# Cosine attention and a feed-forward layer in one kernel: input loads reordered, batch 1's q prepared at once, x in two buffers

## The chip, the cores and the metric

The kernel runs on one core of a Trainium2 chip. The metric is the device time of one execution in microseconds (us). TensorE (PE in the profile) multiplies matrices, VectorE (DVE) and ScalarE (ACT) do elementwise work, GpSimd (POOL) here only issues transfers, and SyncE (SP) issues DMA transposes. Weight loads of TensorE have a row of their own (PEld).

## The reference

```python
def phi(x, c, s):                       # x: (batch, head, seq, 64)
    r = np.maximum(x, 0.0)
    return np.concatenate([r * c, r * s], axis=-1)
q_p = phi(q, cos_w, sin_w)              # cos_w, sin_w depend on the position alone
k_p = phi(k, cos_w, sin_w)
kv  = np.einsum('bhsf,bhsd->bhfd', k_p, v)
z   = np.sum(k_p, axis=2)
num = np.einsum('bhsf,bhfd->bhsd', q_p, kv)
den = np.einsum('bhsf,bhf->bhs', q_p, z)[..., None] + 1e-06
attn = num / den
...
x = attn.transpose(0, 2, 1, 3).reshape(8 * 576, 512)
h = x @ w_in                            # (4608, 512) @ (512, 2048)
g = h * (1.0 / (1.0 + np.exp(-1.702 * h)))
out = g @ w_out                         # (4608, 2048) @ (2048, 512)
```

There are 8 batches of 8 heads with 576 positions of 64 values. All inputs and the output are float32 in memory; the kernel computes in bfloat16 with float32 sums.

## The kernel before

The 4,608 tokens are worked on in nine blocks of 512 (`i`). Each block multiplies by `w_in` (mm1, 16 groups `fc`), applies the activation, and multiplies by `w_out` (mm2). Beside block `i` the attention of batch `i + 1` is done in small pieces, at places given by `at(n, ...)`, where `n` counts 32 steps of a block: 16 of mm1, then 16 of mm2. A batch has 576 rows, so five pieces: four "mains" of 128 rows, that come in one transfer, and a "tail" of 64 rows, in a transfer of its own. Transfers that change the type from float32 to bfloat16 go through GpSimd's queue (the "cast queue"):

```python
    def load_main(b, n):
        state[b][n] = t = two.tile([128, 2048], BF16, name=n)
        nc.gpsimd.dma_start(out=t.rearrange("p (h e) -> p h e", h=H),
                            in_=SRC[n][b, :, 0:512, :].rearrange("h (p c) d -> p h (c d)", c=4))

    def load_tail(b, n, on=None, dt=BF16):
        state[b][n, 4] = t = two.tile([64, 512], dt, name=n + "t" + str(dt == F32))
        (on or nc.gpsimd).dma_start(out=t.rearrange("p (h d) -> p h d", h=H),
                                    in_=SRC[n][b, :, 512:576, :].rearrange("h p d -> p h d"))
    # ... (load_w_in(g), load_w_out(g): quarter g of w_in or w_out, 1 MB of float32, on the cast queue)
    load_tail(0, "k", nc.sync, F32)
    load_tail(0, "v", nc.sync, F32)
    load_main(0, "q")
    # ... (index patterns on GpSimd between the loads)
    load_main(0, "k")
    load_main(0, "v")
    for g in range(4):
        load_w_in(g)
    load_main(1, "q")
    load_tail(1, "q")
    load_tail(0, "q")
    load_w_out(0)
    for n in "kv":
        load_main(1, n)
        load_tail(1, n)
    for g in range(1, 4):
        load_w_out(g)
    load_all(2)                     # q, k and v of batch 2, mains and tails
```

Each piece of q is prepared by VectorE into `qn` and turned by a DMA transpose into `qT`; the tail of batch 0 has a place of its own, `qT_tail`. `unit_kv` makes the small matrix of a batch, `unit_num` the rows of x of one piece in `xb`, and `turn_x` turns them by a DMA transpose into `xT`, which mm1 reads. `qn`, `qT`, `xT`, `kp` and `vt` have one buffer:

```python
    def prep_new(b):
        state[b]["qn"] = one.tile([128, NC, H, 2 * D], BF16, name="qn")
        state[b]["xb"] = one.tile([128, NC, H, D], BF16, name="xb")

    def prep(b, n, c):
        o = state[b]["qn"] if n == "q" else kp
        for cs, w in enumerate((cosw, sinw)):
            nc.vector.tensor_scalar(o[:rows(c), c, :, cs * D:cs * D + D], part(b, n, c), 0.0, w[:rows(c), c:c + 1],
                                    op0=MAX, op1=MUL)
    # ...
    def turn_q(b, c):
        nc.sync.dma_start_transpose(out=q_slot(b, c)[:, :, 0:rows(c)],
                                    in_=state[b]["qn"][:rows(c), c].rearrange("p h e -> p (h e)"))

    def turn_x(b, c):
        nc.sync.dma_start_transpose(out=xT[:, :, ds(b * S + c * 128, rows(c))],
                                    in_=state[b]["xb"][:rows(c), c].rearrange("p h d -> p (h d)"))
    # ...
    def unit_num(b, c):
        nm = at_tile()
        for h in range(H):
            nc.tensor.matmul(nm[:, h // 4, ds(h % 4 * (D + 1), D + 1)], q_slot(b, c)[:, h, :],
                             state[b]["kvs"][:, h // 4, h % 4, 0:D + 1], start=True, stop=True)
        # ... den and inv from nm, on VectorE
        nc.vector.tensor_tensor(state[b]["xb"][:r, c].rearrange("p (n h) d -> p n h d", n=2), nm4[:, :, :, 0:D],
                                inv[:r].unsqueeze(3).to_broadcast([r, 2, 4, D]), op=MUL)
```

Batch 0 is prepared before the first block, with transposes of q and x on TensorE for the four mains, and with matmuls on a constant tile (`warmup`) while TensorE waits. Then follows the loop. In block 0 mm2 goes through the four quarters of `w_out` in turn, each for the four token tiles, so that it can begin with the first quarter:

```python
    warmup(18)
    # ... q of batch 0: prepared, turned on TensorE through two `at` banks, copied to qT by ScalarE
    for c in (4, 0, 1, 2, 3):
        prep(0, "k", c)
    for c in (4, 0, 1, 2, 3):
        prep_v(0, c)
    warmup(14)
    unit_kv(0)
    # ... unit_num(0, 0..3), x turned on TensorE, the first four groups of mm1 of block 0
    for i in range(NBLK):
        # ...
        if i == 0:
            at(4, prep, 0, "q", 4)
            at(4, turn_q, 0, 4)
            at(9, unit_num, 0, 4)
            at(9, turn_x, 0, 4)
        elif i + 2 < B:
            at(1, load_all, i + 2)
        if b < B:                                   # b = i + 1
            k0, k1, k2 = (5, 17, 19) if i == 0 else (0, 12, 17)
            at(k0, prep_new, b)
            for c in range(NC):
                at(k0 + c // 2, prep, b, "q", c)
                at(k0 + c // 2, turn_q, b, c)
                at(k0 + 5 + c // 2, prep, b, "k", c)
                at(k0 + 9 + c // 3, prep_v, b, c)
            at(k1, unit_kv, b)
            for c in range(NC):
                at(k2 + 2 * c, unit_num, b, c)
                at(k2 + 2 * c, turn_x, b, c)
        for n in range(32):
            if n < FC:                              # FC = 16
                if i > 0 or n > 3:
                    mm1(i, n)
            elif i == 0:
                mm2(i, n % 4, (n - FC) // 4)        # token tile, quarter of w_out
            # ...
            else:
                mm2(i, (n - FC) // 4, n % 4)
            for f in work[n]:
                f()
```

Of the kernel before, what the change touches and what calls it, by code (L numbers as in the profile page):

```python
# [9 lines left out]
F32 = mybir.dt.float32  # L10
BF16 = mybir.dt.bfloat16
# [10 lines left out]
def kernel(  # L22
# [9 lines left out]
    nc = tc.nc  # L32
    B, H, S, D = q.shape
# [6 lines left out]
    NC = 5  # L40
# [3 lines left out]
    one = ctx.enter_context(tc.tile_pool(name="one", bufs=1))  # L44
    two = ctx.enter_context(tc.tile_pool(name="two", bufs=2))
# [7 lines left out]
    def rows(c):  # L53
        return 128 if c < 4 else 64
# [4 lines left out]
    def mm_tile():  # L59
        return ps.tile([128, TB], F32, name="mm", bufs=4)  # L60

    def at_tile():
        return ps.tile([128, 2, 512], F32, name="at", bufs=2)

    def warmup(n):
        for _ in range(n):
            wps = mm_tile()
            nc.tensor.matmul(wps, warm[:, 0:128], warm, start=True, stop=True)  # L68


    state = {b: {} for b in range(B)}
    SRC = {"q": q, "k": k, "v": v}

    def load_main(b, n):
        state[b][n] = t = two.tile([128, 2048], BF16, name=n)
        nc.gpsimd.dma_start(out=t.rearrange("p (h e) -> p h e", h=H),
                            in_=SRC[n][b, :, 0:512, :].rearrange("h (p c) d -> p h (c d)", c=4))

    def load_tail(b, n, on=None, dt=BF16):
        state[b][n, 4] = t = two.tile([64, 512], dt, name=n + "t" + str(dt == F32))  # L80
        (on or nc.gpsimd).dma_start(out=t.rearrange("p (h d) -> p h d", h=H),  # L81
                                    in_=SRC[n][b, :, 512:576, :].rearrange("h p d -> p h d"))

    def load_all(b):
        for n in "qkv":
            load_main(b, n)
            load_tail(b, n)
# [6 lines left out]
    def load_w_in(g):  # L94
        nc.gpsimd.dma_start(out=w_in_sb[:, :, ts(g, 512)], in_=win_r[:, :, ts(g, 512)])

    def load_w_out(g):
        nc.gpsimd.dma_start(out=w_out_sb[:, ts(g, 4), :], in_=wout_r[:, ts(g, 4), :])

    pos_i = const.tile([128, NC], I32)  # L100
    id_i = const.tile([128, 128], I32)
    load_tail(0, "k", nc.sync, F32)
    load_tail(0, "v", nc.sync, F32)
    load_main(0, "q")
    nc.gpsimd.iota(pos_i[:, 0:4], pattern=[[1, 4]], base=0, channel_multiplier=4)
    nc.gpsimd.iota(pos_i[:, 4:5], pattern=[[1, 1]], base=512, channel_multiplier=1)
    load_main(0, "k")
    nc.gpsimd.iota(id_i, pattern=[[1, 128]], base=0, channel_multiplier=-1)
    load_main(0, "v")
    for g in range(4):  # L110
        load_w_in(g)
    load_main(1, "q")
    load_tail(1, "q")
    load_tail(0, "q")
    load_w_out(0)
    for n in "kv":
        load_main(1, n)
        load_tail(1, n)
    for g in range(1, 4):
        load_w_out(g)  # L120
    load_all(2)

# [6 lines left out]
    qT = one.tile([128, H, NC * 128], BF16, name="qT")  # L129
# [9 lines left out]
    ident = const.tile([128, 128], BF16)  # L139
# [11 lines left out]
    def part(b, n, c):  # L151
        if c < 4:
            return state[b][n].rearrange("p (h c d) -> p c h d", c=4, d=D)[:, c]
        return state[b][n, 4].rearrange("p (h d) -> p h d", d=D)

    def prep_new(b):
        state[b]["qn"] = one.tile([128, NC, H, 2 * D], BF16, name="qn")
        state[b]["xb"] = one.tile([128, NC, H, D], BF16, name="xb")

    def prep(b, n, c):  # L160
        o = state[b]["qn"] if n == "q" else kp
# [4 lines that stand above are left out]
    def prep_v(b, c):  # L166
        nc.vector.tensor_copy(vt[:rows(c), c, :, 0:D], part(b, "v", c))

    def q_slot(b, c):

        return qT_tail if (b, c) == (0, 4) else qT[:, :, ts(c, 128)]
# [4 lines that stand above are left out]
# [6 lines left out]
    def unit_kv(b):  # L182
        kv = at_tile()
        for h in range(H):
            o = kv[:, h // 4, ds(h % 4 * (D + 1), D + 1)]
            for c in range(NC):
                nc.tensor.matmul(o, kp[:, c, h, :], vt[:, c, h, 0:D + 1], start=(c == 0), stop=(c == NC - 1))  # L187
        kvs = two.tile([128, 2, 4, VW], BF16, name="kvs")
        for n in range(2):
            o, i = kvs[:, n, :, 0:D + 1], kv[:, n, 0:4 * (D + 1)].rearrange("p (h e) -> p h e", h=4)  # L190
            if b == 0 and n == 1:
                nc.scalar.copy(o, i)
            else:
                nc.vector.tensor_copy(o, i)  # L194
        state[b]["kvs"] = kvs
# [28 lines left out]
    def mm1(i, fc):  # L224
        hps = mm_tile()
        mm1_part(hps, i, fc)
        gelu(hps, fc)
# [17 lines left out]
    def mm2(i, t, part):  # L245

        if part == 0:
            cur[t] = mm_tile()
        yps = cur[t]
        for fc in range(part * 4, part * 4 + 4):  # L250
            nc.tensor.matmul(yps, gT[fc][:, ds(t * 128, 128)], w_out_sb[:, fc, :],  # L251
                             start=(fc == 0), stop=(fc == FC - 1))
        if part == 3 and (i > 0 or t < 3):
            evac(i, t)
# [10 lines left out]
    def mm2_last(i, t):  # L265

        yps = mm_tile()
        ysb = ypool.tile([128, d_model], F32, name="ysb")
        hd = d_model // 2
        for n in range(2):  # L270
            cols = ds(n * hd, hd)
            if n == 1:
                yps = mm_tile()
            for fc in range(FC):
                nc.tensor.matmul(yps[:, 0:hd], gT[fc][:, ds(t * 128, 128)], w_out_sb[:, fc, cols],  # L275
                                 start=(fc == 0), stop=(fc == FC - 1))
            if n == 0:
                nc.scalar.copy(ysb[:, cols], yps[:, 0:hd])
            else:
                nc.vector.tensor_copy(ysb[:, cols], yps[:, 0:hd])  # L280
            for m, (p0, cnt, row, step) in enumerate(pieces(i * 4 + t)):
                (nc.sync if m == 0 else nc.scalar).dma_start(out=out[row:row + (cnt - 1) * step + 1:step, cols],
                                                             in_=ysb[p0:p0 + cnt, cols])


    prep_new(0)
    s0 = state[0]
    warmup(18)
    for c2 in range(2):
        tp = at_tile().bitcast(BF16)  # L290
        for c in (2 * c2, 2 * c2 + 1):
            prep(0, "q", c)
            for h in range(H):
                nc.tensor.transpose(tp[:, c % 2, ts(h, 128)], s0["qn"][:, c, h, :], ident)
            nc.scalar.copy(qT[:, :, ts(c, 128)], tp[:, c % 2].rearrange("p (h t) -> p h t", h=H))
    for c in (4, 0, 1, 2, 3):
        prep(0, "k", c)
    for c in (4, 0, 1, 2, 3):
        prep_v(0, c)
    warmup(14)  # L300
    unit_kv(0)
    tp = [mm_tile().bitcast(BF16) for _ in range(2)]

# [25 lines left out]
    for i in range(NBLK):  # L329
        work = {n: [] for n in range(32)}  # L330
        b = i + 1

        def at(n, f, *a):
            work[n].append(lambda: f(*a))

        if i == 0:
            at(4, prep, 0, "q", 4)
            at(4, turn_q, 0, 4)
            at(9, unit_num, 0, 4)
            at(9, turn_x, 0, 4)  # L340
        elif i + 2 < B:
            at(1, load_all, i + 2)
        if b < B:
            k0, k1, k2 = (5, 17, 19) if i == 0 else (0, 12, 17)
            at(k0, prep_new, b)
            for c in range(NC):
                at(k0 + c // 2, prep, b, "q", c)
                at(k0 + c // 2, turn_q, b, c)
                at(k0 + 5 + c // 2, prep, b, "k", c)
                at(k0 + 9 + c // 3, prep_v, b, c)  # L350
            at(k1, unit_kv, b)
            for c in range(NC):
                at(k2 + 2 * c, unit_num, b, c)
                at(k2 + 2 * c, turn_x, b, c)
        for n in range(32):
            if n < FC:
# [3 lines that stand above are left out]
                mm2(i, n % 4, (n - FC) // 4)  # L360
            elif i == NBLK - 1 and n >= 28:
                if n == 28:
                    mm2_last(i, 3)
# [5 lines that stand above are left out]
            evac(i, 3, nc.vector)  # L369
# [30 lines left out]
```

## Time and profile before

The median of three runs is 315.57 us (315.48 to 317.07).

| of the profile | value |
|---|---|
| span of the profiled execution | 315.0 us |
| PE busy | 286.2 us, 91% |
| DVE, ACT, POOL busy | 103.5, 115.9, 97.3 us |
| mm1 (line 216) | 128.5 us |
| mm2 (line 251) | 128.7 us |
| mean granted TensorE clock | 0.973 |
| cast queue (q0) | 43,904 packets, 27.40 MB |
| sync queue (q1) | 52,672 packets, 12.99 MB |

The profile counts a line of idle time to what ended it. "PE at L200 <- DVE den L206: 8.0, 1, 8.0" says that TensorE, before it wrote the tile `at` on line 200, waited 8.0 us in total, once, 8.0 us at the longest, for an instruction of VectorE on line 206. A transfer appears as "DMA out<-in". In the list of DMA queues, q0 is the cast queue and q1 the sync queue, each with packets, megabytes moved, and the share of time of 16 DMA engines. `qtFalse` in the profile is the tail of q in bfloat16, `ktTrue` and `vtTrue` are the two float32 tails of batch 0. The granted clock is a share of full speed.

### The profile page before, as it was taken

What the parts mean: (1) busy time and instruction counts of PE and PEld (TensorE: products, weight loads), DVE (VectorE), ACT (ScalarE), POOL (GpSimd) and SP (SyncE); (2) the same over time, 40 slices, a digit from 0 to 9 for tenths busy, and PEclk for the clock granted to TensorE, in tenths of its full rate; (3) what the DMA queues carried; (4) which work ended last, traced back from release to release, by engine and by line L of the source; (5) the groups of instructions that cost most, each with busy time, mean ns of one, the idle gap of its engine ahead of it and who ended that gap; (6) DMA issues with size and microseconds to landing.
All of it is one profiled execution on the core that took longest, in us unless ns stands there. A gap on an engine that the chain in (4) does not pass through costs nothing.

```text
span 315.0 us, 4917 instructions
## 1 busy us (share of the span) xinstructions
PE 286.2 (91%) x1867; PEld 143.6 (46%) x1900; DVE 103.5 (33%) x347; ACT 115.9 (37%) x193; POOL 97.3 (31%) x115
## 2 busy tenths in 40 slices
PE   7479697089997999999999999999999999999994
PEld 2356252044553455445544554455445544444443
DVE  2851370057435602740472048015902500000000
ACT  4516330006521463155216512641363146316511
POOL 8633420008011941291049015701610220011021
PEclk9998798779999999999999999999999999999999
DMA  7999999937999999599869977995750640011023
GB/s 104 201 206 195 191 190 165 152 69 181 138 149 185 148 156 170 127 203 172 131 116 186 178 116 140 196 177 100 149 113 0 121 89 0 32 70 34 0 62 73
DMA packets 96759, 40.83 MB, mean 130 GB/s; under 512 B 65568, under 2 KB 94496, under 8 KB 96736
## 3 DMA queue, kind: packets, MB, share of 16 engines
q0 software_dynamic: 43904, 27.40, 58.3%
q1 hardware_dynamic: 52672, 12.99, 28.8%
q8 instruction: 15, 0.25, 0.3%
q10 hardware_dynamic: 160, 0.13, 0.1%
q14 instruction: 8, 0.07, 0.1%
HBM read 36.70 MB, written 9.44 MB: 146 GB/s over the span
## 4 chain that ended last, share of the span: by engine, by line
PE 72%; DMA 18%; SPq 3%; DVE 3%; ACT 1%; issue 1%; POOL 0%; DVEq 0%; ACTq 0%; POOLq 0%
PE mm L251 34%; PE mm L216 33%; DMA qtFalse<-in_q_dram 5%; DMA qT<-qn 4%; SPq L174 3%; PE at L200 3%; DMA k<-in_k_dram 3%; DMA xT<-xb 3%; DMA qT_tail<-qn 2%; PE at L187 2%; DVE qn L163 1%; ACT g L221 1%; PE mm L275 1%; DVE kp L163 1%; DVE xb L208 0%
## 5 line engine op out<-in xcount | busy, mean ns | idle before, releaser
L216 PE MATMUL mm<-xT,w_in_sb 128*128 128x512 bf16 (+1 forms) x571 | 128.5, 380 | 0.9
L251 PE MATMUL mm<-w_out_sb,g 128*128 128x512 bf16 x544 | 128.7, 384 | 0.7 <-issue 0.2
L263 POOL DMA_DIRECT2D out_dram<-ysb x54 | 50.4, 937 | 192.9 <-ACT ysb L261 192.5
L221 ACT ACTIVATE g<-mm 128x512 bf16<-128x512 f32 x144 | 85.8, 597 | 51.5 <-PE mm L216 51.5
L216 PEld LDWEIGHTS <-w_in_sb 128*128 128x128 bf16 x588 | 57.9, 99 | 66.2 <-issue 1.8
L251 PEld LDWEIGHTS <-g 128*128 128x128 bf16 x560 | 52.8, 99 | 59.2 <-issue 2.7
L261 ACT COPY ysb<-mm 128x512 f32<-128x512 f32 x34 | 19.9, 587 | 125.2 <-PE mm L251 125.2
L208 DVE TENSOR_TENSOR xb<-at,inv 128x512 bf16<-128x512 f32 (+1 forms) x40 | 27.6, 690 | 15.4 <-DMA xT<-xb 13.8
L200 PE MATMUL at<-kvs,qT 128*128 128x65 bf16 x312 | 16.6, 196 | 12.9 <-DVE den L206 8.0
L194 DVE CAST kvs<-at 128x260 bf16<-128x260 f32 x15 | 5.8, 426 | 60.9 <-PE at L187 60.9
L200 PEld LDWEIGHTS <-qT 128*128 128x128 bf16 x312 | 14.8, 99 | 22.5 <-issue 9.1
L206 DVE TENSOR_SCALAR den<-at 128x8 f32<-128x8 f32 (+1 forms) x40 | 6.5, 163 | 50.0 <-PE at L200 50.0
L280 DVE COPY ysb<-mm 128x256 f32<-128x256 f32 x1 | 0.4, 425 | 59.4 <-PE mm L275 59.4
L163 DVE TENSOR_SCALAR qn<-q,cosw 128x512 bf16<-128x512 bf16 x32 | 11.0, 343 | 12.1 <-DMA qT_tail<-qn 7.4
L163 DVE TENSOR_SCALAR qn<-q,sinw 128x512 bf16<-128x512 bf16 x32 | 11.9, 371 | 0.0
L187 PEld LDWEIGHTS <-kp 128*128 128x128 bf16 x320 | 10.7, 97 | 1.9
L163 DVE TENSOR_SCALAR kp<-k,sinw 128x512 bf16<-128x512 bf16 x32 | 11.5, 359 | 0.0
L187 PE MATMUL at<-vt,kp 128*128 128x65 bf16 x320 | 11.0, 193 | 0.0
L163 DVE TENSOR_SCALAR kp<-k,cosw 128x512 bf16<-128x512 bf16 x32 | 10.9, 340 | 0.0
L68 PE MATMUL mm<-warm 128*128 128x512 bf16 x32 | 9.3, 455 | 1.2 <-DVE warm L57 1.2
L81 POOL DMA_DIRECT2D qtFalse<-in_q_dram x8 | 8.7, 1089 | 4.6 <-DMA k<-in_k_dram 4.1
L207 DVE RECIPROCAL inv<-den 128x8 f32<-128x8 f32 (+1 forms) x40 | 8.1, 202 | 1.4
(52 smaller groups left out, 92.3 us busy)
## 6 DMA issues: line engine op xcount, KB each, us to landing
out_dram<-ysb POOLq DMA_DIRECT2D x38, 128.0 KB, 3.2
q<-in_q_dram POOLq DMA_DIRECT2D x8, 512.0 KB, 9.7
k<-in_k_dram POOLq DMA_DIRECT2D x8, 512.0 KB, 11.1
v<-in_v_dram POOLq DMA_DIRECT2D x8, 512.0 KB, 12.6
out_dram<-ysb POOLq DMA_DIRECT2D x16, 256.0 KB, 2.9
w_in_sb<-in_moe_w_in_dram POOLq DMA_DIRECT2D x4, 512.0 KB, 14.6
w_out_sb<-in_moe_w_out_dram POOLq DMA_DIRECT2D x4, 512.0 KB, 15.5
xT<-xb SPq DMA_TRANSPOSE x36, 3.0
```

Source lines behind the costliest of these rows:

```text
L68: nc.tensor.matmul(wps, warm[:, 0:128], warm, start=True, stop=True)
L81: (on or nc.gpsimd).dma_start(out=t.rearrange("p (h d) -> p h d", h=H), in_=SRC[n][b, :, 512:576, :].rearrange("h p d -> p h d"))
L163: nc.vector.tensor_scalar(o[:rows(c), c, :, cs * D:cs * D + D], part(b, n, c), 0.0, w[:rows(c), c:c + 1], op0=MAX, op1=MUL)
L174: nc.sync.dma_start_transpose(out=q_slot(b, c)[:, :, 0:rows(c)], in_=state[b]["qn"][:rows(c), c].rearrange("p h e -> p (h e)"))
L187: nc.tensor.matmul(o, kp[:, c, h, :], vt[:, c, h, 0:D + 1], start=(c == 0), stop=(c == NC - 1))
L200: nc.tensor.matmul(nm[:, h // 4, ds(h % 4 * (D + 1), D + 1)], q_slot(b, c)[:, h, :], state[b]["kvs"][:, h // 4, h % 4, 0:D + 1], start=Tru ...
L208: nc.vector.tensor_tensor(state[b]["xb"][:r, c].rearrange("p (n h) d -> p n h d", n=2), nm4[:, :, :, 0:D], inv[:r].unsqueeze(3).to_broadca ...
L216: nc.tensor.matmul(hps[:, c0:c1], w_in_sb[:, kc, ds(fc * 128, 128)], xT[:, kc, ds(i * TB + c0, c1 - c0)], start=(kc == 0), stop=(kc == KC ...
L221: nc.scalar.activation(g, hps, AF.Gelu_apprx_sigmoid)
L251: nc.tensor.matmul(yps, gT[fc][:, ds(t * 128, 128)], w_out_sb[:, fc, :], start=(fc == 0), stop=(fc == FC - 1))
L261: nc.scalar.copy(ysb, cur[t])
L263: nc.gpsimd.dma_start(out=out[row:row + (n - 1) * step + 1:step, :], in_=ysb[p0:p0 + n, :])
```

## The change

Four things are changed. All transfers of the inputs now go through the cast queue, the three tails of batch 0 right behind its three mains. The loads of batch 1 (q, k, v) stand between the groups of `w_in`, and all of `w_out` comes after them. The tail of q of batch 0 is turned before the first block, and the q of batch 1 is prepared at the beginning of block 0, so that its transposes can start early. And `xb` gets a second buffer, so that the x of one batch need not have been turned when the next batch's begins. The q transposes of batch 0 on TensorE go through four one-bank tiles instead of two double ones, and there are 7 fewer warm-up matmuls.

```diff
-    def load_tail(b, n, on=None, dt=BF16):
+    def load_tail(b, n):
         # ... always on the cast queue, always to BF16
-    load_tail(0, "k", nc.sync, F32)
-    load_tail(0, "v", nc.sync, F32)
     load_main(0, "q")
     # ...
     load_main(0, "k")
     # ...
     load_main(0, "v")
-    for g in range(4):
-        load_w_in(g)
+    for n in "kvq":
+        load_tail(0, n)
+    load_w_in(0)
     load_main(1, "q")
     load_tail(1, "q")
-    load_tail(0, "q")
-    load_w_out(0)
-    for n in "kv":
-        load_main(1, n)
-        load_tail(1, n)
-    for g in range(1, 4):
+    load_w_in(1)
+    load_w_in(2)
+    load_main(1, "k")
+    load_tail(1, "k")
+    load_w_in(3)
+    load_main(1, "v")
+    load_tail(1, "v")
+    for g in range(4):
         load_w_out(g)
     load_all(2)
 # ...
-        state[b]["xb"] = one.tile([128, NC, H, D], BF16, name="xb")
+        state[b]["xb"] = two.tile([128, NC, H, D], BF16, name="xb")
 # ...
-    warmup(18)
-    for c2 in range(2):
-        tp = at_tile().bitcast(BF16)
-        for c in (2 * c2, 2 * c2 + 1):
-            prep(0, "q", c)
-            for h in range(H):
-                nc.tensor.transpose(tp[:, c % 2, ts(h, 128)], s0["qn"][:, c, h, :], ident)
-            nc.scalar.copy(qT[:, :, ts(c, 128)], tp[:, c % 2].rearrange("p (h t) -> p h t", h=H))
-    for c in (4, 0, 1, 2, 3):
+    warmup(13)
+    for c in range(4):
+        tp = mm_tile().bitcast(BF16).rearrange("p (h t) -> p h t", h=H)
+        prep(0, "q", c)
+        for h in range(H):
+            nc.tensor.transpose(tp[:, h], s0["qn"][:, c, h, :], ident)
+        nc.scalar.copy(qT[:, :, ts(c, 128)], tp)
+    for c in range(NC):
         prep(0, "k", c)
-    for c in (4, 0, 1, 2, 3):
+    for c in range(NC):
         prep_v(0, c)
-    warmup(14)
+    prep(0, "q", 4)
+    turn_q(0, 4)
+    warmup(12)
     unit_kv(0)
 # ...
         if i == 0:
-            at(4, prep, 0, "q", 4)
-            at(4, turn_q, 0, 4)
-            at(9, unit_num, 0, 4)
-            at(9, turn_x, 0, 4)
+            at(2, unit_num, 0, 4)
+            at(2, turn_x, 0, 4)
 # ...
-            k0, k1, k2 = (5, 17, 19) if i == 0 else (0, 12, 17)
+            k0, k1, k2 = (0, 16, 18) if i == 0 else (0, 12, 17)
             at(k0, prep_new, b)
             for c in range(NC):
-                at(k0 + c // 2, prep, b, "q", c)
-                at(k0 + c // 2, turn_q, b, c)
-                at(k0 + 5 + c // 2, prep, b, "k", c)
-                at(k0 + 9 + c // 3, prep_v, b, c)
+                at(k0, prep, b, "q", c)
+                at(k0 + c, turn_q, b, c)
+                at(k1 - 7 + c // 2, prep, b, "k", c)
+                at(k1 - 3 + c // 3, prep_v, b, c)
```

More of the change, by code (lines that the diff above doesn't have):

```diff
@@ L77, in load_main @@
                             in_=SRC[n][b, :, 0:512, :].rearrange("h (p c) d -> p h (c d)", c=4))
-    def load_tail(b, n, on=None, dt=BF16):
-        state[b][n, 4] = t = two.tile([64, 512], dt, name=n + "t" + str(dt == F32))
-        (on or nc.gpsimd).dma_start(out=t.rearrange("p (h d) -> p h d", h=H),
-                                    in_=SRC[n][b, :, 512:576, :].rearrange("h p d -> p h d"))
+    def load_tail(b, n):
+        state[b][n, 4] = t = two.tile([64, 512], BF16, name=n + "t")
+        nc.gpsimd.dma_start(out=t.rearrange("p (h d) -> p h d", h=H),
+                            in_=SRC[n][b, :, 512:576, :].rearrange("h p d -> p h d"))
     def load_all(b):
```

## The prediction

> **What bounds the kernel now.** I read, in this order: the page, a table by stretches of time, the lists of who waited for whom on TensorE and VectorE, the chain of waits, and the DMA queues in short windows. The page says PE busy 91%, so at most some 9% is idle, and the question is where. The stretches (columns: length, busy time of each engine with instruction counts, granted clock, DMA share, GB/s) are cut at the first matmul of token block 0, at its first mm2, and at the first matmuls of blocks 1, 2 and 3:
>
> ```profile
> 23.40:43.20 19.80, 17.10 (x89) 9.11 (x90) 8.07 (x27) 9.92 (x17) 8.22 (x10) 0.85 1.43 195
> 43.20:72.90 29.70, 19.27 (x144) 9.23 (x145) 6.90 (x23) 2.35 (x4) 1.14 (x2) 0.83 1.02 133
> 72.90:104.90 32.00, 30.01 (x205) 14.90 (x208) 18.39 (x58) 11.32 (x19) 10.35 (x13) 1.00 1.29 165
> 104.90:135.10 30.20, 29.99 (x206) 15.04 (x209) 12.41 (x44) 11.90 (x20) 12.95 (x14) 1.00 1.10 154
> ```
>
> Block 2 takes 30.2 us with PE busy 29.99: that is TensorE's own work for a block that also prepares the next batch. Block 1 takes 32.0, block 0 takes 49.5 (23.4 to 72.9). So block 0 loses about 19.4 us, block 1 about 1.8, and from 104.9 on nothing can be won. The waits of TensorE between 33 and 75 us, then VectorE's longest one:
>
> ```profile
> PE at L200 <- DVE den L206: 8.0, 1, 8.0
> PE at L200 <- DMA qT_tail<-qn: 2.6, 1, 2.6
> PE at L200 <- DMA qT<-qn: 2.2, 2, 2.0
> ```
>
> ```profile
> DVE xb L208 <- DMA xT<-xb: 13.8, 1, 13.8
> ```
>
> The three PE waits are 12.8 us. The rest of the 19.4, about 6.6 us, is the reduced clock (0.85 and 0.83 above) that surrounds them. The longest wait is a buffer wait: `xb` has one buffer, so batch 1's first `xb` waits until batch 0's last piece has been turned. The chain of waits (start, length, what) shows why that comes so late:
>
> ```profile
> 11.62 16.72 DMA qtFalse<-in_q_dram
> ...
> 29.00 7.21 DMA qT_tail<-qn
> ...
> 44.30 3.74 SPq L174
> ...
> 48.15 4.15 SPq L174
> ...
> 54.34 8.53 DMA xT<-xb
> ```
>
> The q tail of batch 0 lands at 28.3, behind four weight groups; its transpose lands at 36.2, the one `qn` buffer holds up batch 1's q until then, five transposes follow on the sync queue, and the tail's `xT` transpose is behind them.
>
> Last, what the transfers cost: the DMA queues in 9 to 12 us (q, k, v), 15 to 19 us (weights) and 58 to 61 us (k, v and transposes together).
>
> ```profile
> q0 software_dynamic: 1175, 0.59, 145.6%
> ```
>
> ```profile
> q0 software_dynamic: 836, 0.82, 124.1%
> ```
>
> ```profile
> q0 software_dynamic: 742, 0.37, 89.1%
> q1 hardware_dynamic: 739, 0.18, 46.9%
> ```
>
> Alone, a 512 B packet of a q, k or v main costs 3/1175 = 2.55 ns and a 1 KB weight packet 4/836 = 4.8 ns. A main has 1024 packets and a weight group 512, so each is about 2.6 us. A tail's 512 packets took about 0.6 us (847 packets in 26 to 27 us). Beside transposes the queues advance packet for packet, 742 to 739, at 4.04 ns a pair: **each transpose packet costs the load stream 1.5 ns**. I count 1024 packets for a q piece, 512 for a q tail or an x piece, 256 for an x tail.
>
> **What the skill says.** "DMA: Bandwidth & Descriptors", Queues, rings and completion order: each DMA engine takes packets in turn from the queue rows that have work. The 742 and 739 agree. The same page, Issuing engines are not separate DMA queues: transfers of any engine share the same 16 DMA engines, so moving two tails from sync to the cast queue makes no bandwidth. "TensorE: Matmul & The Clock Gate", Part 1: after an idle window of about 3.4 us the clock halves until a busy window has passed; after the 8.0 us wait the window 60 to 65 us shows 0.50. "SBUF — State Buffer", SBUF: two separate sides: VectorE in a two-port mode keeps GpSimd from writing descriptors; the load of batch 0's q tail beside copies and casts took 3.70 us to issue against 0.69 for others. So tails issued amid preparation can be slow to start, but the queue then still holds several loads.
>
> **The change, part by part.** No compute is removed except 7 warm-up matmuls; the same bytes move.
>
> *Start.* The two f32 tails leave the sync queue. They moved 1,053 packets before 7 us (530 to 4 us, 523 from 4 to 7), 1.5 ns each: the first q lands 1.6 us earlier than its 8.6 (issue at 1.28, landing 7.3), at 7.0. In steps of 2.6 and 0.6: k 9.7, v 12.3, tails of k, v, q 12.9, 13.5, 14.1. VectorE then needs 0.5 for the k tail and 1.2 for the v copies: unit_kv at about 15.4 against 17.2, so block 0's matmuls start about 1.8 us earlier, near 21.7. The four q transposes no longer wait for `at` banks; that lies inside the wait for k and v.
>
> *Load order.* w_in 0 16.7, q1 19.3, its tail 19.9, w_in 1 22.5. The q tail of batch 0 is turned from about 16 on, lands near 23 and adds 0.8: w_in 1 23.3, w_in 2 25.9, k1 28.5. Batch 1's q can be prepared once `qn` is free (23), so its transposes are issued from 24; issue to first packets under load I take as 4 us, since a lone q-tail transpose took 7.2 and its 512 packets 2 to 3 of them. From 28 on every load packet pays 1.5 ns more: k1 tail 29.9, w_in 3 33.3, v1 37.4, its tail 38.8, **w_out 0 42.2**, 45.6, 49.0, **w_out 3 52.4**. The transposes that pass (512+512+1024+512+4x512 = 4,608 packets) are exactly batch 1's five q pieces.
>
> *TensorE in block 0.* The wait of 2.6 for `qT_tail` goes (it lands at 23, needed at 27). Before, the first mm1 part started at 23.5, the four prologue groups were through at 28.5 (part of it at the lowered clock), and each further group of four matmuls took 0.86. Shifted by 1.8 and with 0.4 for the tail's unit_num, group 4 starts at 27.1 and group 12 at 34: w_in 3 is there at 33.3, and mm1 ends near 37.5. Then mm2 needs w_out 0, and it is not there until 42.2: **a new wait of about 5 us**, long enough to lower the clock for one window (1.7 us lost). unit_kv(1) cannot fill it, being placed after the first mm2. From 42.2: 64 matmuls 13.8, unit_kv 1.4, five unit_num 1.3, 1.7 for the clock: 60.4.
>
> *x in two buffers.* The 13.8 us wait of VectorE and the 8.0 of TensorE go. But block 1 also needs x pieces 0 to 3 of batch 1 turned. Their 2,048 packets stand behind the q pieces (done near 54) and pass beside batch 2's q, tail and half of k: 4.1 + 1.4 + 2.1 = 7.6 us, so near 62. By the other route, unit_num(1,3) follows nine groups of mm2 (7.8), unit_kv (1.4), three unit_num (0.8) and the clock's 1.7 after 42.2, so at about 54.2; with 1.1 for VectorE and a landing of 7 to 8 under load (xT transposes at 91 to 96 us: median 7.3), it is 62.5 to 63.5. **Block 1 starts at 62.7** instead of 72.9, a gain of 10.2.
>
> *Block 1 on.* The 1.8 us wait there was for q pieces beside batch 3's loads; these loads now follow batch 2's closely, but the transposes are issued relatively earlier. I count half, 0.9, as gained, and take back 0.5 for a start after a wait. Sum: 315.6 - 10.2 - 0.9 + 0.5 = **305.0 us**.
>
> **Rivals.** (a) The loads are hidden and block 0 runs without a wait: first matmul 21.7, block 1 at about 54, time near 297. Against it: bytes ahead of w_out 0 grew by k1, v1 and three tails, and DMA share already is 1.43 through block 0. (b) `xb` does it all and the new order costs as much as it saves: with the old order the 8.0 us and its clock loss alone would give some 8 to 10 us, so near 306, which the total cannot tell from mine; the wait before the first mm2 can. (c) The x transposes come later still, or a second idle stretch keeps the clock at half: block 1 at 66 to 67, time near 309. For it: landings of 9 to 14 us for q transposes under load. (d) Slower than before would need over 10 us of new waits beyond the 5 counted; nothing in the profile offers them.
>
> **Range and chances.** The sum of load times is checked by the trace of before (w_in 0 to 2 and the next main landing 2.5 to 3.2 us apart), so w_out 0 is good to 2 us; the x landing to 3. Range 301.0 to 309.0. Faster by over 2% means under 309.3: 0.90; same 0.08; slower 0.02.
>
> **What would show it.** TensorE waiting 3 to 7 us for w_out 0 before its first mm2 near 42; no wait of VectorE's `xb` on xT; a wait of 1 to 3 us for xT at block 1's first mm1 near 63; clock under 1 around both; blocks 2 to 6 unchanged at 30.1. I am wrong if w_out 0 lands before 38 (then near 300), or if block 1 starts after 67.

## The result and the profile after

The changed kernel takes 308.71 us (median of four runs, 306.78 to 308.90) against 316.32 us of the kernel before, measured beside it. The ratio is 0.9743, with a 95% interval of 0.9688 to 0.9798: 2.6% faster. The profiled executions have spans of 307.0 and 315.0 us.

The same table of stretches as before (length, busy time of each engine with instruction counts, granted clock, DMA share, GB/s), cut again at the first matmul of block 0, its first mm2, and the first matmuls of blocks 1, 2 and 3:

```profile
22.90:43.00 20.10, 15.22 (x89) 8.21 (x88) 9.31 (x30) 10.51 (x18) 6.25 (x7) 0.92 1.38 180
43.00:65.20 22.20, 18.80 (x143) 10.06 (x146) 9.14 (x27) 1.76 (x3) 5.18 (x8) 0.88 1.36 178
65.20:97.10 31.90, 31.59 (x204) 15.47 (x210) 14.34 (x51) 11.32 (x19) 9.25 (x10) 0.95 1.23 182
97.10:127.10 30.00, 29.79 (x206) 14.89 (x208) 12.21 (x43) 11.91 (x20) 12.76 (x14) 1.00 1.23 154
```

Block 0 is 42.3 us long (22.9 to 65.2) where it was 49.5, and begins 0.6 us earlier (22.91 against 23.49). Block 1 begins at 65.2 instead of 72.9 and is as long as it was (31.9 against 32.0), block 2 takes 30.0. So 7.7 of the 8.0 us that the span lost lie before 65.2. The longest waits of TensorE from 24 to 110 us, then those of VectorE from 43 to 75 us:

```profile
PE mm L252 <- DMA w_out_sb<-in_moe_w_out_dram: 4.8, 1, 4.8
PE mm L217 <- issue: 3.1, 1, 3.1
```

```profile
DVE kvs L195 <- PE at L188: 6.9, 1, 6.9
DVE den L207 <- PE at L201: 5.4, 5, 2.0
DVE ysb L260 <- PE mm L252: 3.2, 1, 3.2
```

The waits for `qT_tail`, for q pieces and for `den` are gone, and VectorE's `xb` waits no more for `xT`. In their place stand a wait of 4.8 us for the first quarter of `w_out`, before mm2, and one of 3.1 us before the first mm1 of block 1, which the list calls "issue". The chain of waits (start, length, what) says what it is:

```profile
21.20 21.76 DMA w_out_sb<-in_moe_w_out_dram
42.96 0.05 issue
43.01 1.89 PE mm L252 x4
...
54.99 8.72 DMA xT<-xb
63.71 1.48 issue
65.19 0.38 PE mm L217
```

The load of `w_out`'s first quarter lands at 42.96, and 0.05 us later mm2 begins. The x transpose issued at 54.99 is piece 2 of batch 1, and it lands at 63.71. Piece 3 is issued at 56.97 and takes 8.0 us to land, so it is there at about 65.0. So mm1 stood for piece 3 until 65.19, and the 1.48 us of "issue" is part of that wait.

Block 1 keeps its length for another reason than before. The wait for a q piece in it is gone, but it starts at half clock after the 3.1 us wait: its mean clock is 0.95, and (1 - 0.95) x 31.9 = 1.6 us. (In 65 to 68.5 us the granted clock is 0.58, in block 2 it is 1.00.)

### The profile page after: what moved, and what is told of

It is laid out like the page before. It is cut to its first block, busy times and chain, and to the rows that moved or that the text cites. A ratio compares the mean times of both kernels' runs of the same rounds, so it can differ in the third digit from the quotient of the medians.

```text
span 307.0 us, 4893 instructions
## 1 busy us (share of the span) xinstructions
PE 285.4 (93%) x1860; PEld 144.3 (47%) x1893; DVE 104.4 (34%) x347; ACT 115.8 (38%) x193; POOL 97.6 (32%) x117
## 4 chain that ended last, share of the span: by engine, by line
PE 81%; DMA 14%; POOL 2%; issue 1%; DVE 0%; POOLq 0%; DVEq 0%
PE mm L252 37%; PE mm L217 36%; DMA w_out_sb<-in_moe_w_out_dram 7%; DMA q<-in_q_dram 4%; PE at L188 3%; DMA xT<-xb 3%; PE at L201 3%; PE mm L276 1%; POOL vt L81 0%; POOL q L76 0%; POOL k L76 0%; POOL v L76 0%; POOL w_in_sb L95 0%; POOL kt L81 0%; POOL qt L81 0%
## 5 line engine op out<-in xcount | busy, mean ns | idle before, releaser
L201 PEld LDWEIGHTS <-qT 128*128 128x128 bf16 x312 | 15.7, 101 | 9.0 <-issue 0.6
L188 PE MATMUL at<-vt,kp 128*128 128x65 bf16 x320 | 12.6, 199 | 1.6 <-DVE vt L168 1.6
L188 PEld LDWEIGHTS <-kp 128*128 128x128 bf16 x320 | 12.0, 102 | 4.3 <-issue 2.5
L164 DVE TENSOR_SCALAR kp<-k,cosw 128x512 bf16<-128x512 bf16 x32 | 11.8, 368 | 1.0 <-DMA k<-in_k_dram 0.9
L76 POOL DMA_DIRECT2D k<-in_k_dram x8 | 8.8, 1098 | 5.8 <-DMA v<-in_v_dram 5.8
L168 DVE COPY vt<-v 128x512 bf16<-128x512 bf16 x32 | 7.8, 303 | 4.5 <-DMA v<-in_v_dram 4.5
L68 PE MATMUL mm<-warm 128*128 128x512 bf16 x25 | 7.5, 447 | 1.6 <-DVE warm L57 1.2
## 6 DMA issues: line engine op xcount, KB each, us to landing
w_out_sb<-in_moe_w_out_dram POOLq DMA_DIRECT2D x4, 512.0 KB, 22.4
```

## The experiments

All are compared with the kernel before, run on the same chip. The columns are the median time, the ratio with its interval, the start and length of block 1 (from the first mm1 of blocks 1 and 2), and TensorE's waits of 1 us or more between 24 us and the end of block 1. The last two columns come from one profiled execution of each kernel, and the executions of one kernel differ by up to 3 us (300.5 to 303.7 in one case), so a difference of that size in these columns alone shows nothing.

| kernel | us | ratio (95%) | block 1 from, us long | waits, us |
|---|---|---|---|---|
| before | 316.3 | | 72.9, 32.0 | `den` 8.0, `qT_tail` 2.6, q pieces 4.0 |
| after | 308.7 | 0.9743 (0.9688-0.9798) | 65.2, 31.8 | `w_out` 4.8, x 3.1 |
| before with `xb` in two buffers | 309.6 | 0.9780 (0.9762-0.9798) | 66.8, 31.4 | q pieces 5.2, `qT_tail` 2.4 |
| after with `xb` in one buffer | 308.0 | 0.9721 (0.9690-0.9752) | 65.3, 31.5 | `w_out` 6.2, x 3.0 |
| after, load order of before | 314.1 | 0.9891 (0.9847-0.9935) | 68.5, 32.6 | v 6.9, x 4.1, q pieces 1.5 |
| after, float32 tails on sync | 308.4 | 0.9709 (0.9665-0.9753) | 65.2, 30.1 | `w_out` 3.4, x 3.5, q piece 1.0 |
| after, batch 2's loads held | 308.3 | 0.9734 (0.9706-0.9761) | 61.6, 33.5 | `w_out` 6.3, q pieces 2.6 |
| the same, and batch 3's held | 303.6 | 0.9585 (0.9561-0.9608) | 60.7, 30.4 | `w_out` 6.4 |
| after, batch 1's q turned on TensorE | 301.5 | 0.9537 (0.9490-0.9584) | 59.2, 31.5 | x 2.9 |
| that, with the load order of before | 301.7 | 0.9526 (0.9504-0.9549) | 59.3, 30.1 | x 1.8, q copy 1.0 |
| that, and x of batch 1 on TensorE | 301.9 | 0.9510 (0.9475-0.9545) | 60.0, 30.1 | `xb` 1.8 in five |
| that, and batch 2's loads held | 302.4 | 0.9527 (0.9486-0.9568) | 55.6, 35.1 | q pieces 3.2, x 1.1 |
| that, and batches 2's and 3's held | 299.3 | 0.9476 (0.9453-0.9500) | 55.6, 31.5 | none (0.7 for v) |

"That" in the last four rows is the kernel with batch 1's q on TensorE and the new load order, unless the row says otherwise.

### The second buffer alone, and everything but the second buffer

The kernel before with one line changed:

```diff
-        state[b]["xb"] = one.tile([128, NC, H, D], BF16, name="xb")
+        state[b]["xb"] = two.tile([128, NC, H, D], BF16, name="xb")
```

> The kernel before with one line changed: xb in two buffers, loads and all else as before. My theory: the 13.8 us wait of VectorE's xb on xT goes, but batch 1's q pieces still land at 48 to 62 us, so TensorE waits for them instead and the x pieces of batch 1 stand behind them; block 1 starts near 67 instead of 72.9, time about 310 us (309 to 312). Rival 'the second buffer does it all and the new load order is neutral': 308.5 us or less, block 1 at 65 or earlier. Rival 'the wait was only shown there, the q transposes were the limit': 314 us or more.

Measured 309.6 us, block 1 from 66.8. Its waits of TensorE (24 to 110 us):

```profile
PE at L200 <- DMA qT<-qn: 5.2, 3, 2.2
PE at L200 <- DMA qT_tail<-qn: 2.4, 1, 2.4
PE mm L216 <- DMA xT<-xb: 0.8, 1, 0.8
```

The 8.0 us wait is gone and waits for q pieces take part of its place, as expected. This one line alone brings 7 us, nearly as much as the whole change. The opposite, the kernel after with that line undone:

> The kernel after with xb in one buffer again. My theory: the tail of x of batch 0 is now turned at 42.8 us, before batch 1's first xb is written at 50.3, so the second buffer is idle in the new order: time as after, within 0.5 us (308 to 309), and no wait of xb on xT. Rival 'the second buffer is what the change gained': 314 to 317 us with a wait of xb on xT of several us.

Measured 308.0 us, the same as the kernel after within the intervals. VectorE's waits in it from 40 to 75 us:

```profile
DVE kvs L195 <- PE at L188: 7.0, 1, 7.0
DVE den L207 <- PE at L201: 5.0, 5, 1.3
DVE ysb L260 <- PE mm L252: 3.2, 1, 3.2
DVE vt L168 <- DMA vt<-in_v_dram: 2.2, 2, 1.5
```

No `xb` on `xT`, with one buffer. So the second buffer and the early tail are two cures of one wait, and each alone is enough: in the new order the tail of x was turned long before batch 1's first `xb`.

### The load order

The kernel after, with the loads behind batch 0's tails in the order of before:

```diff
-    load_w_in(0)
-    load_main(1, "q")
-    ...
+    for g in range(4):
+        load_w_in(g)
+    load_main(1, "q")
+    load_tail(1, "q")
+    load_w_out(0)
+    for n in "kv":
+        load_main(1, n)
+        load_tail(1, n)
+    for g in range(1, 4):
+        load_w_out(g)
```

> The kernel after with the load order of before behind batch 0's tails: four w_in groups, batch 1's q and its tail, w_out 0, batch 1's k and v with tails, w_out 1 to 3. My theory: the order only moves the wait. w_out 0 is there when mm1 ends, and TensorE waits about 3.5 us for w_out 1 instead, which lands as late as in the kernel after; batch 1's q lands 8 us later and its pieces are turned 2 us later, so the x pieces too: block 1 near 67, time 309 to 311 us, 1 to 2 us above the kernel after. Rival 'the new order is the gain': 313 us or more. Rival 'the new order costs': below 307 us.

Measured 314.1 us: my theory missed, and the rival of "the new order is the gain" had the number. TensorE's waits (24 to 110 us), then VectorE's instructions on v:

```profile
PE at L186 <- DVE vt L166: 6.9, 2, 4.4
PE mm L215 <- issue: 4.1, 1, 4.1
PE at L199 <- DMA qT<-qn: 1.5, 1, 1.5
```

```profile
41.45 0.90 DVE L166 COPY vt<-v 128x512 bf16<-128x512 bf16 x4 [3.18 <-DMA v<-in_v_dram]
44.78 0.29 DVE L166 COPY vt<-vt 64x512 bf16<-64x512 bf16 x1 [2.44 <-DMA vt<-in_v_dram]
```

I had looked for the wait at the second quarter of `w_out`. It is at unit_kv, which TensorE meets one step after mm2's start and which needs batch 1's v. In this order v's tail comes in for a copy at 44.78 where the new order has it at 39.90, and 1.5 us more is lost at q pieces, 1 us more at x. With all else changed, the new load order is worth about 5 us (314.1 against 308.7; by the two ratios, 1.5% of 316 us).

The tails at the start, the kernel after with the first two lines of loads of before:

```diff
+    load_tail(0, "k", nc.sync, F32)
+    load_tail(0, "v", nc.sync, F32)
     load_main(0, "q")
 # ...
-    for n in "kvq":
-        load_tail(0, n)
+    load_tail(0, "q")
```

> The kernel after with the float32 tails of k and v of batch 0 on the sync queue at the very start, as before. My theory: the same bytes go through the same DMA engines, so w_out 0 lands within 0.7 us of the kernel after (43.0) and the time is the same within 1 us (307.5 to 309.5), though the first q lands 1 to 1.6 us later. Rival 'the start is worth its 1.6 us': 310 us or more.

Measured 308.4 us, with mm2's start at 42.30 against 43.01. As expected: which queue carries these two tails makes no difference here.

### The transposes beside the loads

The kernel after, with the five q pieces of batch 1 turned on TensorE:

```diff
+    def turn_q_pe(b, c):
+        r = rows(c)
+        tq = mm_tile().bitcast(BF16).rearrange("p (h t) -> p h t", h=H)
+        for h in range(H):
+            nc.tensor.transpose(tq[:, h, 0:r], state[b]["qn"][:r, c, h, :], ident[:r, :r])
+        nc.vector.tensor_copy(q_slot(b, c)[:, :, 0:r], tq[:, :, 0:r])
 # ...
-                at(k0 + c, turn_q, b, c)
+                if i == 0:
+                    at((4, 6, 8, 10, 12)[c], turn_q_pe, b, c)
+                else:
+                    at(k0 + c, turn_q, b, c)
```

> The kernel after, with the five q pieces of batch 1 turned on TensorE in mm1 of block 0 (40 more matmuls, about 2.5 us of TensorE, five copies on VectorE) and not by DMA. My theory: each transpose packet costs the load stream 1.5 ns, so without the 3,072 that passed before w_out 0 it lands 4.6 us earlier, near 38.4, and w_out 3 near 46; the wait of 4.8 us before the first mm2 shrinks to 0 to 1, block 1 starts at 58 to 60, time 302 to 304 us. Rival 'transposes and loads do not slow each other, the load stream has its own pace': w_out 0 still at 42 to 43, time 307 to 309 us.

Measured 301.5 us, 7 us below the kernel after, though TensorE has 40 matmuls more. The first quarter of `w_out`, issued at 20.50, lands 18.0 us later at 38.5, against 42.96: 4.5 us earlier, where 4.6 were expected. The last quarter lands at 46.2 (29.36 + 16.8) against 52.8 (29.61 + 23.2): 6.6 earlier. This is no chance of one execution: in the four kernels with this load order and q on TensorE the first quarter lands at 38.3 to 38.7, in the five with q turned by DMA at 42.3 to 43.5.

The agreement with 1.5 ns is looser than 4.5 and 4.6 look. This execution led by 0.4 us before any transpose of batch 1's q had begun (the third group of `w_in` lands at 26.27 against 26.67). And between 24 us and the landing of the first quarter 2,634 packets passed on the sync queue in the kernel after and 316 in this one: 2,318 fewer, not 3,072. That is 4.1 us and 1.8 ns a packet. Up to the last quarter it is 4,294 and 316 packets, 6.2 us and 1.6 ns. The DMA queues in 42 to 45 us (packets, MB, share), first of the kernel after, then of this one:

```profile
q0 software_dynamic: 478, 0.48, 93.1%
q1 hardware_dynamic: 478, 0.11, 29.9%
```

```profile
q0 software_dynamic: 679, 0.61, 125.6%
```

Beside transposes the load queue moves as many packets as the sync queue does, and fewer than it moves alone. Whether the cost goes by packets or by bytes these runs do not separate: all transpose packets are of one size, and their 1.0 MB at the 0.61 MB in 3 us that the loads move alone would be 4.9 us of the 6.2.

The chain of waits of this kernel around the start of mm2 and of block 1:

```profile
37.33 2.70 PE mm L224 x12
40.03 0.86 PE mm L259 x4
...
51.21 7.82 DMA xT<-xb
59.03 0.14 issue
59.17 11.02 PE mm L224 x44
```

mm1 runs into mm2 with no wait. What remains is the wait for x piece 3, 7.82 us from issue to landing. The load order of before was then tried again with q on TensorE (its five places two steps later, at 6 to 14):

> The load order of before behind batch 0's tails, with batch 1's q turned on TensorE (two steps later, since its q lands later). My theory: the old order cost 6 us only because its v and w_out landed beside the q transposes; without them v's tail lands near 38.4 and w_out 1 near 41, ahead of their use at 40.9 and 44.5, so the order is nearly free: 301 to 303 us, within 1.5 us of the run with the new order and q on TensorE. Rival 'the new order is better by itself': 305 us or more.

Measured 301.7 us, equal to the new order. So the 5 us that the load order is worth exist only while batch 1's q is turned by DMA: without these transposes v's tail lands at 39.3 in the old order, not at 44.8.

### The wait at the start of block 1

Two ways to take it away. The first holds batch 2's loads until x piece 3 of batch 1 is written, by a small copy on GpSimd that reads it:

```diff
-    load_all(2)
+    hold = const.tile([128, 8], BF16)
+    def load_after_x(b, c):
+        nc.gpsimd.tensor_copy(hold, state[b]["xb"][:, c, 0, 0:8])
+        load_all(b + 1)
 # ... in block 0, behind unit_num(1, 3)
+                at(24, load_after_x, 1, 3)
```

> The kernel after, with the loads of batch 2 held on the cast queue until x piece 3 of batch 1 has been written (a copy of 8 columns on GpSimd that reads it). My theory: the x transposes of batch 1 then find the DMA engines free, land about 3 us after issue instead of 7 to 9, the 3.1 us wait at the first mm1 of block 1 and the half clock after it go: block 1 at 62 to 62.5 instead of 65.2 and 30.1 us long instead of 31.9; time 303.5 to 305 us. Rival 'that wait is not for the x transposes, or the held loads come too late for batch 2': time 308 us or more, with new waits in block 1.

Measured 308.3 us: block 1 starts at 61.6 as expected, but the time misses the 303.5 to 305 and is that of the kernel after; the rival had the number, and its new waits. TensorE's longest waits (24 to 110 us):

```profile
PE mm L256 <- DMA w_out_sb<-in_moe_w_out_dram: 6.3, 1, 6.3
PE at L205 <- DMA qT<-qn: 2.6, 2, 1.4
```

Of the 3.6 us won at the start of block 1, 1.7 go back within it: 33.5 us instead of 31.8, with 2.6 us of waits for batch 2's q pieces. In this execution 2.0 us are left (block 2 begins at 95.0 against 97.0), but it is the shortest of its four (306.9 us) and that of the kernel after the longest (308.9); by the medians nothing is left, and where the other three lost it no trace shows. The held loads end later and run into batch 3's, and batch 2's q transposes stand beside both. If that is so, holding batch 3's loads as well must free it (a copy that reads batch 2's `kvs`, near the middle of block 1, ahead of `load_all(3)`):

> As the run with batch 2's loads held, and batch 3's loads held too, until batch 2's kvs is written (a copy of 8 columns on GpSimd; near 75 us). My theory: what that run lost again in block 1 (2.6 us waiting for q pieces, 0.3 for x) came from batch 3's loads and the output stores running beside batch 2's q transposes; with batch 3's loads later the q pieces pass alone: block 1 starts near 61.6 as there and is 30.1 to 30.8 us long instead of 33.5; time 304 to 305.5 us. Rival 'the q pieces are late because batch 2's own loads are late': waits of 2 us or more for q pieces remain, time 307 us or more.

Two of the four executions, the profiled one among them, were disturbed (604.4 and 313.5 us); the other two took 303.6 and 303.4 us, a ratio of 0.9597 (0.9578 to 0.9616), and the kernel was run once more:

> The kernel with batch 2's and batch 3's loads held once more, for an undisturbed profile. As before: block 1 from about 61.6, 30.1 to 30.8 us long, no wait of 1 us or more for q pieces; 303 to 305 us. Rival: waits of 2 us or more for q pieces, 307 us or more.

Measured 303.6 us, ratio 0.9585. Its waits of TensorE (24 to 110 us):

```profile
PE mm L260 <- DMA w_out_sb<-in_moe_w_out_dram: 6.4, 1, 6.4
PE mm L225 <- DMA w_in_sb<-in_moe_w_in_dram: 0.4, 1, 0.4
```

No wait of block 1 for x or q pieces is left, and block 1 is 30.4 us long. The second way turns batch 1's x on TensorE, on top of q:

```diff
+    def turn_x_at(b, c):
+        r = rows(c)
+        o = at_tile().bitcast(BF16)[:, 0, 0:KC * r].rearrange("p (kc t) -> p kc t", kc=KC)
+        for kc in range(KC):
+            nc.tensor.transpose(o[:, kc], state[b]["xb"][:r, c, 2 * kc:2 * kc + 2, :].rearrange("p h d -> p (h d)"),
+                                ident[:r, :r])
+        nc.scalar.copy(xT[:, :, ds(b * S + c * 128, r)], o)
 # ... in block 0, one step behind unit_num(1, c), in place of turn_x(1, c)
+                    at(k2 + 2 * c + 1, turn_x_at, b, c)
```

> As the run with batch 1's q turned on TensorE, and the x pieces of batch 1 too (20 more matmuls of TensorE, about 1.3 us, each one step after its unit_num; copies on ScalarE, which is idle there). My theory: after the q pieces the last wait of block 0 is that of 2.9 us for the x transposes beside batch 2's loads, with a half clock after it. It goes: block 1 at 57.5 to 58 instead of 59.2 and 30.1 us long instead of 31.5, time 298 to 299.5 us. Rival 'batch 2's loads are too late for an earlier block 1': new waits in block 1 for q pieces or k and v, time 301 us or more.

Measured 301.9 us, no gain over q alone: a miss. The wait is gone and block 1 takes 30.1, but it starts at 60.0:

```profile
PE at L189 <- DVE xb L224: 1.8, 5, 0.4
```

One step is too short for VectorE to finish `xb`, so the five pieces cost 1.8 us of waits. From the first mm2 to block 1 TensorE is also busy 1.9 us longer (18.32 against 16.45 us), where 1.3 were expected for the matmuls. Together that is 3.7 us, nearly the 2.9 of the x wait and the 1.4 of the half clock that it saved. And the holds on top of q on TensorE, first batch 2's, then batch 2's and 3's:

> As the run with batch 1's q turned on TensorE, and batch 2's loads held until x piece 3 of batch 1 is written. My theory from the held loads alone, where the wait moved into block 1: the x transposes land at once, block 1 starts at 56.5, but batch 2's q pieces are turned beside batch 2's and batch 3's loads, and 2 to 3 us of waits come back in block 1; time 300 to 302 us, no more than 1 us from the run without the hold. Rival 'with the load stream 4 us earlier there is room for it': no wait in block 1, time 297 to 298.5 us.

> Batch 1's q turned on TensorE, batch 2's and batch 3's loads both held. My theory: block 1 starts near 55.6 and is 30.1 to 30.8 us long instead of 35.1, time 297.5 to 299 us, the shortest of all. Rival as in the run before this one: waits for q pieces of batch 2 remain in block 1, time 301 us or more.

Measured 302.4 and 299.3 us, each 0.3 to 0.4 above its range. With the first, block 1 starts at 55.6 and is 35.1 us long: the wait moves into block 1 again. With both it starts at 55.6 and is 31.5 long (cut at 21.5, 55.6 and 87.1 us):

```profile
21.50:55.60 34.10, 33.89 (x268) 19.25 (x271) 16.89 (x51) 12.21 (x21) 7.81 (x11) 0.96 1.07 162
55.60:87.10 31.50, 30.19 (x204) 14.98 (x207) 17.78 (x61) 11.64 (x20) 12.20 (x17) 1.00 1.42 200
```

In block 0 TensorE is busy 33.89 of 34.10 us. This version is 5.2% below the kernel before and the shortest of all; block 1, expected 30.1 to 30.8 us long, kept 1.3 us of idle time.

## Why the prediction was right, and where its sizes were off

The time, 308.7 us, is inside the range of 301 to 309, near its upper end, and 3.7 us above the estimate of 305.0. Of these, 0.7 are the base (the prediction started from 315.6, the four runs of before have 316.3) and 3.0 are gain that did not come: 7.6 us instead of 10.6. The signs named beforehand came: a wait of 4.8 us for `w_out` before the first mm2, no wait of `xb` on `xT`, a wait of 3.1 us before block 1, the clock under 1 around both, later blocks as before.

**Load stream.** The step that mattered held: the new order puts `w_out` behind batch 1's loads and transposes, and mm2 waits for it. The first quarter was predicted at 42.2 and landed at 42.96; the new wait was "about 5 us" and is 4.8. That it came so close is in part luck, since two errors had opposite signs. The loads were 0.8 us late before any q transpose of batch 1 moved (k of batch 1 at 29.33, not 28.5). The transposes then came later than thought: the q tail of batch 0 was turned at 25.4, not 23, the first q piece was issued at 26.24 and its first packets moved at 30.2, not 28, so that 2,634 packets had passed at 42.96 where 3,072 were counted. The cost of a transpose packet, put at 1.5 ns, was tested by taking the transposes away: 1.6 to 1.8 ns.

**x in two buffers.** The wait went, as said, but it was put under the wrong part: it went with one buffer too. In the new order the early tail removes it. The old wait has two cures, and the sum counted it only once, so the total was not touched.

**Block 1's start** was 62.7 in the prediction and is 65.2. This term of the sum is where most of the difference lies. `w_out` is 0.8 late. The reduced clock after the wait was counted as 1.7 us, but it stayed at half from 43.0 to 48.5, which costs some 2.7:

```profile
43.00:48.00 5.00, 4.77 (x46) 3.25 (x48) 0.77 (x2) 0.00 (x0) 1.57 (x2) 0.50 1.21 195
```

So unit_num(1,3) came at 55.35 instead of 54.2 (the terms of the prediction, added up, give 53.9). x piece 3 was issued 1.6 us after it instead of 1.1, took 8.0 us to land, the upper end of the 7 to 8, and mm1 began 0.2 us later. Nearly all have the same sign. That x pieces beside batch 2's loads are the limit there was right: with those loads held, block 1 started at 61.6 and 60.7.

**Block 1.** Half of its old wait, 0.9, was counted as gained, and 0.5 as lost to a start after a wait. All of the wait, 1.8, went, but the half clock took 1.6: 0.1 us shorter where 0.4 was counted.

**The start.** Block 0's first mm1 was expected 1.8 us earlier and came 0.6 earlier (22.91 against 23.49). The first q did land earlier; VectorE took its first q at 7.48 instead of 8.72. But k, expected at 9.7, came at 11.02, so the tail of k at 14.2 and not 12.9; the four v copies took 1.25 us in place of 0.88, unit_kv started at 15.30 and stopped for v until 16.07, and the clock was 0.54 from 20 to 25 us. Part of this belongs to the one execution: in the nine other kernels that keep this start, k comes at 10.1 to 10.5 and mm1 begins at 21.1 to 22.4, around the 21.7 predicted. It cost nothing in this kernel: with DMA transposes and this load order mm2 waits for `w_out` in any case, and begins at 42.9 to 43.5 in the three of the nine that have both.

**The rivals.** (b), that `xb` does it all and the new order costs as much as it saves, is refuted by what was undone: without the second buffer the time is the same, without the new order it is 5 us longer; that `xb` alone gains 7 us (309.6) is the other cure of the same wait. (a), no wait before mm2, is what turning q on TensorE made: 301.5. (c) was nearest for the time: x came later and the clock stayed at half longer, though it took no second idle stretch; block 1 at 65.2 where it said 66 to 67.

Beside loads an x piece takes 7 to 9 us to land. Two traces say where the time goes. With q on TensorE, x piece 0 of batch 1 is issued at 45.27, with no other transpose before it in its queue. Not one packet of the sync queue moves until 49.3, and the piece lands at 53.07: about 4.1 of the 7.8 us pass before the first packet. With batch 2's loads held as well, the same piece is issued at 44.73, moves from 45.8 and lands at 47.13, after 2.4 us. So most of the difference is delay before the first packet; the "4 us to first packets" that the prediction assumed was right. What holds the first packet back while loads are queued stays open.

## What to carry to other kernels

A wait that a profile shows can have two independent cures, and doing both counts once: undo each part alone before crediting it. Where a stretch is bound by a stream of loads, count everything else that passes through the DMA engines beside it: here 1.0 MB of transposes held up the loads by 6.2 us, and moving them to TensorE, which had been waiting for these loads, was worth nearly as much again as the whole change (7.2 us after 7.6). And a transfer that is put off must be followed to the next place where it meets others: holding the loads of one batch brought waits into the next block and nothing by the median, and only holding the next batch too made it a gain of 5 us.

## What was not expected of the hardware

A wait of 3 us can cost half as much again by the clock that follows, or nothing: after 3.1 us block 1 of the kernel after lost 1.6 us more, while with the float32 tails it waited 3.5 us and was then 30.1 us long, at full clock. Both were single executions, and what decides between them was not tested. And what a part of a change is worth can depend wholly on what stands beside it: the new load order is worth 5 us with DMA transposes beside it and 0 without (301.5 against 301.7).
